# Writing out the slots of a windowed-attention and maxout kernel, each in its own order

## The chip, the cores and the metric

The kernel runs on one core of a Trainium2 chip. A core has five engines that run independently, each through its own instructions in a fixed order: TensorE (PE in the profile, with its weight loads as PEld), VectorE (DVE), ScalarE (ACT), GpSimd (POOL), and SyncE (SP), which here only issues DMAs. An instruction waits, if it must, on semaphores that other engines or DMAs raise, and everything behind it on its engine waits with it. The metric is the time of one execution in microseconds (us); the kernel before takes 179.16 us, the median of three runs (178.92 to 179.60).

## The reference

Two stages are computed one after the other.

```python
# q, k, v: (4 batches, 8 heads, 768 positions, 64); n_sink = 4, window = 128
scores = (q @ k^T) / sqrt(64)
keep = (key < n_sink) | (0 <= query - key < window)
a = softmax(where(keep, scores, -1e9))
x = (a @ v), heads side by side            # (3072 tokens, 512)
h = max(x @ w1, x @ w2, x @ w3)            # (3072, 768)
out = h @ w_out                            # (3072, 512)
```

## The kernel before

**Tiling.** The tokens are cut into twelve chunks of 256, three to a batch. A chunk's queries are two blocks of 128; a block sees the keys of its own block, of the block ahead of it, and the four sinks at the head of the batch. The work on chunk n is written as small helpers, each of which issues a few instructions:

- `load(n, 'k')`, `'q'`, `'v'` issue one DMA of 512 KB each on SP into raw float32 tiles, of which there are two for k, two for q and two for v. A `gate` puts a tiny GpSimd instruction ahead, so that the DMA waits for GpSimd's place in its own order.
- `cast_qk(n, w, g, engine)` casts half of k or q to bfloat16 on the engine named (4 per chunk); `cast_v(n, ...)` casts a quarter of v (4 per chunk).
- `turn(n, w, g)` and `turn2` transpose k or q with TensorE and a copy out of PSUM (chunks 0 to 3); `turn_dma(n, w)` does it with DMA transposes on SP (chunks 4 on; two DMAs for k into `kT`, one for q into `qT`).
- `score(n, pairs)` computes the scores of pairs of heads (four pairs, 0 to 3) into two PSUM banks per pair; `expo(n, p)` is ScalarE's two exponentials of a pair, which free the two banks; `mask(n, p)` multiplies by the 0/1 window mask on VectorE. In the first chunks `premask` lets TensorE write the mask into the bank ahead of the scores, in place of `mask`.
- `sink_k`, `sink_v` gather the sinks' keys (GpSimd) and values (a small TensorE product and a VectorE copy) once per batch; `sink_score(n)` scores them, `av_open(n)` opens the four output banks with the sinks' product. Chunks 0, 3, 6 and 9 need no sinks, since they lie at the head of a batch.
- `av(n, p)` multiplies by v, then VectorE divides by the sum (`rc` and `x_sb`, L359 and L362). `xpose` transposes x with TensorE, `xpose_dma(n)` with one DMA transpose on SP into `xT` (chunk 4 on).
- `ffn_h(n, fp, wi)`: eight matmuls for a third `fp` of h and one matrix `wi`; for `wi` = 0 ScalarE copies the bank into `h_sb` (L401), for 1 and 2 VectorE takes the maximum (L405). `ffn_y(n, t)`: six matmuls of half of the output and a copy, on ScalarE or on VectorE. `store(n)` writes it out.
- `warm(n)` is n matmuls on zeros, at the start.

**Order.** The order is written out by hand: each engine runs its instructions as the program text names them. From chunk 4 on the program runs in slots. I call slot n the stretch in which chunk n's scores are taken. In it TensorE also does the nine `ffn_h` of chunk n-1 and the two `ffn_y` of chunk n-2, while SP loads chunk n+2 and GpSimd casts it. Slots 4 and 11 and the stretch that follows 11 have their own branch in the loop; slots 5, 7, 8 and 10 share one, slots 6 and 9 share another.

**PSUM.** There are eight banks. `bank` takes the one that was freed longest ago in program order, and TensorE waits until whoever freed it is really done.

**The end of an execution** (the last slots) is the same text in both kernels.

Of the kernel before, what the change touches and what calls it, by code (L numbers as in the profile page):

```python
# [16 lines left out]
def kernel(  # L17
# [13 lines left out]
    nc = tc.nc  # L31
# [17 lines left out]
    with tc.manual_schedule():  # L49
# [445 lines left out]
        score(0, (1,))
        premask(1, (1,))
        turn2(1, 'k', 0, nc.vector)
        cast_qk(1, 'k', 1, nc.scalar)
        score(0, (3,))
        expo(0, 1)  # L500
        cast_qk(1, 'q', 1, nc.gpsimd)
        load(1, 'v')
        turn2(1, 'k', 1, nc.scalar)
        expo(0, 3)
        av_open(0)
        av(0, 0)
        av(0, 1)
        sink_v(0)
        turn2(1, 'q', 0, nc.vector)
        load_w(1, 0, 512)  # L510
        turn2(1, 'q', 1, nc.scalar)
        av(0, 2)
        av(0, 3)
        cast_v(1, 1, 1, nc.vector)
        score(1, (0,))
        expo(1, 0)
        sink_score(1)
        cast_v(1, 0, 1, nc.gpsimd)
# [7 lines left out]
        cast_v(1, 0, 0, nc.vector)  # L526
        premask(1, (3,))
        expo(1, 1)
        score(1, (3,))
        ffn_h(0, 2, 0)  # L530
        mask(1, 2)
        load(2, 'k', gate=after(0, 300))
        mask(1, 0)
        load_w(2, 512, 768)
        av_open(1)
        av(1, 2)
        av(1, 1)
        load_w(2, 0, 256)
        expo(1, 3)
        load(2, 'v', gate=after(1))  # L540
        av(1, 0)
        ffn_h(0, 1, 0)
        load(3, 'q', gate=after(0))
        av(1, 3)
        ffn_h(0, 0, 0)
        load_w(2, 256, 512)
        xpose(1, 1, nc.vector)
        xpose(1, 0, nc.scalar)
        ffn_h(0, 2, 1)
        cast_qk(2, 'q', 0, nc.gpsimd)  # L550
        load_wo(0, 3)
        ffn_h(1, 0, 0)
        ffn_h(1, 1, 0)
        load_wo(3, 6)
        ffn_h(1, 2, 0)
        load(3, 'k', gate=after(1))
        ffn_h(1, 0, 1)
        ffn_h(1, 1, 1)
        ffn_h(0, 0, 1)
        ffn_h(0, 1, 1)  # L560
        ffn_h(0, 2, 2)
        load(3, 'v', gate=after(2))
        cast_qk(2, 'k', 1, nc.scalar)
        cast_qk(2, 'k', 0, nc.gpsimd)
        cast_qk(2, 'q', 1, nc.vector)
        ffn_h(1, 2, 1)
        turn(2, 'q', 0, nc.scalar)
        ffn_h(1, 2, 2)
        turn(2, 'q', 1, nc.scalar)
        turn(2, 'k', 1, nc.vector)  # L570
        cast_v(2, 0, 1, nc.gpsimd)
        turn(2, 'k', 0, nc.vector)
        ffn_h(1, 0, 2)
        load(4, 'q')
        sink_score(2)
        score(2, (1,))
        load(4, 'k', gate=after(2))
        cast_v(2, 0, 0, nc.gpsimd)
        score(2, (2,))
        score(2, (3,))  # L580
        expo(2, 3)
        expo(2, 1)
        ffn_h(1, 1, 2)
        ffn_h(0, 0, 2)
        expo(2, 2)
        mask(2, 1)
        ffn_h(0, 1, 2)
        cast_v(2, 1, 1, nc.vector)
        cast_qk(3, 'q', 0, nc.gpsimd)
        cast_v(2, 1, 0, nc.vector)  # L590
        score(2, (0,))
        mask(2, 2)
        expo(2, 0)
        mask(2, 0)
        av_open(2)
        mask(2, 3)
        cast_qk(3, 'q', 1, nc.gpsimd)
        load(4, 'v', gate=pool_gate)
        ffn_y(1, 0)
        ffn_y(0, 0)  # L600
        cast_qk(3, 'k', 0, nc.scalar)
        av(2, 2)
        ffn_y(0, 1, nc.vector)
        av(2, 0)
        turn(3, 'q', 1, nc.scalar)
        turn(3, 'q', 0, nc.scalar)
        av(2, 3)
        av(2, 1)
        cast_qk(3, 'k', 1, nc.scalar)
        turn(3, 'k', 0, nc.scalar)  # L610
        cast_v(3, 1, 0, nc.vector)
        ffn_y(1, 1)
        cast_v(3, 1, 1, nc.gpsimd)
        turn(3, 'k', 1, nc.vector)
        xpose(2, 0, nc.scalar)
        xpose(2, 1, nc.vector)
        score(3, (0,))
        expo(3, 0)
        score(3, (3,))
        score(3, (1,))  # L620
        load(5, 'k')
        expo(3, 1)
        mask(3, 0)
        cast_v(3, 0, 0, nc.gpsimd)
        score(3, (2,))
        cast_v(3, 0, 1, nc.gpsimd)
        cast_qk(4, 'q', 1, nc.gpsimd)
        cast_qk(4, 'k', 1, nc.gpsimd)
        cast_qk(4, 'k', 0, nc.vector)
        ffn_h(2, 1, 0)  # L630
        expo(3, 2)
        expo(3, 3)
        ffn_h(2, 1, 1)
        cast_qk(4, 'q', 0, nc.gpsimd)
        mask(3, 1)
# [260 lines left out]
```

## Time and profile before

| | |
|---|---|
| median of three runs | 179.16 us (178.92 to 179.60) |
| the profiled execution | 179.04 us, its span 177.3 us |
| TensorE busy | 170.1 us, 96% of the span |
| VectorE / ScalarE / GpSimd busy | 126.5 / 85.8 / 67.1 us |
| mean granted TensorE clock | 0.996 |
| a slot (5, 7, 8, 10) | 13.1 to 13.2 us |
| a slot at the head of a batch (6, 9) | 12.5 us |

Busy time here is the time in which an engine has an instruction in hand. The span runs from the first to the last instruction; the time of an execution is some 1.7 us longer. A row of an order of time gives the start, the duration, the engine, the line of the kernel, the operation with output and input tiles and the number of instructions merged into the row; in brackets stand the idle time ahead of it and what ended that.

### The profile page before, as it was taken

What the parts mean: (1) busy time and instruction counts of PE and PEld (TensorE: products, weight loads), DVE (VectorE), ACT (ScalarE), POOL (GpSimd) and SP (SyncE); (2) the same over time, 40 slices, a digit from 0 to 9 for tenths busy, and PEclk for the clock granted to TensorE, in tenths of its full rate; (3) what the DMA queues carried; (4) which work ended last, traced back from release to release, by engine and by line L of the source; (5) the groups of instructions that cost most, each with busy time, mean ns of one, the idle gap of its engine ahead of it and who ended that gap; (6) DMA issues with size and microseconds to landing.
All of it is one profiled execution on the core that took longest, in us unless ns stands there. A gap on an engine that the chain in (4) does not pass through costs nothing.

```text
span 177.3 us, 4632 instructions
## 1 busy us (share of the span) xinstructions
PE 170.1 (96%) x1872; PEld 127.1 (72%) x1872; DVE 126.5 (71%) x267; ACT 85.8 (48%) x171; POOL 67.1 (38%) x123
## 2 busy tenths in 40 slices
PE   6899999999998999999999999999999999999991
PEld 2446889856895597697696696796795895796870
DVE  3389738699698578796884984975885875966451
ACT  3498732577924822913724814814616617320210
POOL 6884344146580274544724624417427000000000
PEclk9999999999999999999999999999999999999998
DMA  5999999995999969999999999999999519305203
GB/s 141 290 287 203 224 248 259 216 265 148 290 140 236 94 142 299 129 245 173 251 269 189 210 301 160 213 303 153 198 293 198 150 34 379 125 11 170 120 0 118
DMA packets 69573, 34.90 MB, mean 197 GB/s; under 512 B 26544, under 2 KB 68016, under 8 KB 69552
## 3 DMA queue, kind: packets, MB, share of 16 engines
q1 hardware_dynamic: 64912, 31.33, 81.3%
q0 software_dynamic: 4496, 3.15, 11.6%
q8 instruction: 14, 0.23, 0.5%
q10 hardware_dynamic: 144, 0.13, 0.2%
q14 instruction: 7, 0.06, 0.1%
HBM read 25.17 MB, written 6.29 MB: 177 GB/s over the span
## 4 chain that ended last, share of the span: by engine, by line
PE 87%; DMA 4%; DVE 3%; SPq 2%; POOL 1%; ACT 1%; issue 0%; POOLq 0%
PE h_ps L394 52%; PE y_ps L415 18%; PE o L354 6%; PE st L278 6%; DMA q_raw<-in_q_dram 4%; SPq L90 2%; DVE h_sb L405 1%; PE o L336 1%; PE sk L304 1%; PE pt L118 1%; PE y_ps L425 1%; DVE x_sb L362 1%; POOL q_bf L102 1%; PE xt L375 1%; DVE vb L108 0%
## 5 line engine op out<-in xcount | busy, mean ns | idle before, releaser
L394 PE MATMUL h_ps<-xT,w 128*128 128x256 bf16 x864 | 100.7, 273 | 0.1
L394 PEld LDWEIGHTS <-w 128*128 128x128 bf16 x864 | 82.2, 98 | 10.4 <-issue 0.5
L405 DVE TENSOR_TENSOR h_sb<-h_sb,h_ps 128x512 bf16<-128x512 bf16 (+1 forms) x74 | 49.2, 671 | 21.2 <-PE h_ps L394 19.4
L290 ACT ACTIVATE e_sb<-st 128x512 bf16<-128x512 f32 (+1 forms) x96 | 46.6, 579 | 5.9 <-PE st L278 5.8
L401 ACT CAST h_sb<-h_ps 128x512 bf16<-128x512 f32 x36 | 21.2, 588 | 43.1 <-PE h_ps L394 42.9
L108 POOL CAST vb<-v_raw 64x512 bf16<-64x512 f32 x38 | 28.0, 737 | 15.8 <-DMA v_raw<-in_v_dram 14.5
L296 DVE TENSOR_TENSOR e_sb<-e_sb,msk 128x1024 bf16<-128x1024 bf16 (+1 forms) x42 | 31.6, 786 | 2.5 <-ACT e_sb L290 2.3
L415 PE MATMUL y_ps<-wo,h_sb 128*128 128x512 bf16 x138 | 32.4, 379 | 0.2 <-DVE h_sb L405 0.2
L415 PEld LDWEIGHTS <-h_sb 128*128 128x128 bf16 x138 | 12.6, 98 | 14.8 <-issue 1.6
L362 DVE TENSOR_TENSOR x_sb<-o,rc 128x256 bf16<-128x256 f32 x48 | 20.4, 425 | 1.6
L102 POOL CAST k_bf<-k_raw 128x512 bf16<-128x512 f32 x17 | 10.3, 625 | 28.5 <-DMA k_raw<-in_k_dram 28.5
L102 POOL CAST q_bf<-q_raw 128x512 bf16<-128x512 f32 x21 | 13.3, 658 | 16.4 <-DMA q_raw<-in_q_dram 13.0
L417 DVE COPY y_sb<-y_ps 128x512 f32<-128x512 f32 x13 | 9.0, 691 | 13.7 <-PE y_ps L415 13.7
L354 PE MATMUL o<-vb,e_sb 128*128 128x65 bf16 x352 | 16.5, 193 | 0.0
L354 PEld LDWEIGHTS <-e_sb 128*128 128x128 bf16 x352 | 14.6, 97 | 2.0 <-DVE e_sb L296 0.2
L278 PE MATMUL st<-qT,kT 64*128 64x128 bf16 (+1 forms) x256 | 14.5, 238 | 0.5 <-ACT kT L125 0.5
L278 PEld LDWEIGHTS <-kT 64*128 64x128 bf16 x256 | 8.1, 94 | 7.1 <-issue 4.9
L310 ACT ACTIVATE e_sink<-sk 128x256 bf16<-128x256 f32 x8 | 3.1, 385 | 14.8 <-PE sk L304 14.8
L359 DVE RECIPROCAL rc<-o 128x4 f32<-128x4 f32 x48 | 8.4, 175 | 1.3 <-PE o L354 1.0
L417 ACT COPY y_sb<-y_ps 128x512 f32<-128x512 f32 x10 | 5.9, 586 | 3.3 <-PE y_ps L415 2.7
L102 ACT CAST k_bf<-k_raw 128x512 bf16<-128x512 f32 x5 | 3.1, 626 | 6.5 <-DMA k_raw<-in_k_dram 6.5
L180 PE MATMUL warm<-wz 128*128 128x512 bf16 x14 | 4.5, 462 | 1.2 <-DVE wz L169 1.2
(69 smaller groups left out, 72.7 us busy)
## 6 DMA issues: line engine op xcount, KB each, us to landing
k_raw<-in_k_dram SPq DMA_DIRECT2D x12, 512.0 KB, 5.5
q_raw<-in_q_dram SPq DMA_DIRECT2D x12, 512.0 KB, 7.0
v_raw<-in_v_dram SPq DMA_DIRECT2D x12, 512.0 KB, 8.2
out_dram<-y_sb SPq DMA_DIRECT2D x11, 512.0 KB, 4.0
w<-in_moe_w_dram POOLq DMA_DIRECT2D x5, 256.0 KB, 8.7
w<-in_moe_w_dram POOLq DMA_DIRECT2D x2, 512.0 KB, 9.8
wo<-in_moe_w_out_dram POOLq DMA_DIRECT2D x2, 384.0 KB, 9.8
kT<-k_bf SPq DMA_TRANSPOSE x16, 3.7
```

The costliest lines, as they stand in the source:

```text
L102: f(x[:, 2 * g:2 * g + 2].rearrange("q p i a d -> q p a i d"), y[:, 4 * g:4 * g + 4].rearrange("q (p a) i d -> q p a i d", a=2))
L108: eng.tensor_copy(vb[ci % RING][64 * i:64 * i + 64, n, :, 0:D], raws[ci, "v"][64 * n:64 * n + 64, :, i])
L278: nc.tensor.matmul(st[a][:, s:s + q1 - q0].rearrange("q n (i r) -> q n i r", i=2), lhsT=x[hp, n, p].rearrange("q i r -> q (i r)"), rhs=qc[ ...
L290: nc.scalar.activation(e[:, a, lo:], st[a][:, lo:], AF.Exp, scale=scale)
L296: (eng or nc.vector).tensor_mul(e[:, :, lo:], e[:, :, lo:], msk0 if lo else msk)
L354: nc.tensor.matmul(o[:, t, a], lhsT=e[:, a, s], rhs=vb[cv % RING][:, n, 2 * p + a], start=first, stop=True, skip_group_check=True)
L362: nc.vector.tensor_mul(xs[ci][:, :, p], o[:, :, :, 0:D], rc.unsqueeze(3).to_broadcast([128, 2, 2, D]))
L394: nc.tensor.matmul(hp[:, f].rearrange("q (i t r) -> q i t r", i=2, t=2), lhsT=w_sb[wi][:, ds, c0:c0 + 128], rhs=xTs[ci][:, :, ds].rearrang ...
L401: nc.scalar.copy(dst, hp)
L405: nc.vector.tensor_max(dst[:, x], dst[:, x], hp[:, x])
L415: nc.tensor.matmul(yp, lhsT=hs[ci][:, fb, t * 128:(t + 1) * 128], rhs=wo[:, fb], start=(fb == 0), stop=(fb == FB - 1))
L417: (nc.scalar.copy if eng is None else eng.tensor_copy)(ys[ci][:, t], yp)
```

## The change

Nothing that is computed changes, apart from four more `warm` matmuls (18 in place of 14). The order changes in four ways.

1. **Opening and chunks 0 to 3.** The helpers are called in another order. Twelve `warm` stand at the start and six after the last scores of chunk 0 (4, 9 and 1 before). `load(0, 'q')` has no gate now; `load(1, 'k')` is issued third, ahead of `load(0, 'v')`. Several casts of chunks 1 to 3 change their engine, and `load(4, 'k')` and `load(4, 'q')` change places.
2. **Slots 4 to 10 are written out.** The loop is gone. Before, all eight casts of the chunk ahead are on GpSimd. Now each has its place and engine: in slots 5, 7 and 8 three of the q and k casts are on ScalarE and one on VectorE, in slots 6 and 9 two on ScalarE, one on VectorE and one on GpSimd; the v casts stay on GpSimd there. Slot 4 casts both chunk 5 and chunk 6.
3. **Transfers.** The loads stay at the head of their slot, but what follows them is no longer `xpose_dma(n)`: in slots 5, 7, 8 and 10 it stands between the k and the q transposes of the chunk just loaded, in slots 6 and 9 behind both, and the store, which stood at the end of a slot, stands behind the loads.
4. **The sinks' v product**, `sink_v`, moves from slots 6 and 9 to slots 7 and 10, just ahead of their `sink_score`; `sink_k` moves to the end of slots 6 and 9.

SP's queue, slot 5 before. The numbers behind `kT` and `qT` are those of the ring of four tiles, so `kT_72` and `qT_76` belong to chunk 7 and `kT_69` and `qT_73` to chunk 8; `xT` is chunk 5's:

```order
L90 DMA k_raw<-in_k_dram 128x8x128
L90 DMA q_raw<-in_q_dram 128x8x128
L90 DMA v_raw<-in_v_dram 128x8x128
L381 DMA_TRANSPOSE xT<-x_sb 128x8x128
L162 DMA_TRANSPOSE kT_72<-k_bf 128x8x64 x2
L157 DMA_TRANSPOSE qT_76<-q_bf 128x8x128
L431 DMA out_dram<-y_sb 128x1024
```

SP's queue after, from the store of slot 5 to the end of slot 6:

```order
L431 DMA out_dram<-y_sb 128x1024
L162 DMA_TRANSPOSE kT_72<-k_bf 128x8x64 x2
L381 DMA_TRANSPOSE xT<-x_sb 128x8x128
L157 DMA_TRANSPOSE qT_76<-q_bf 128x8x128
L90 DMA k_raw<-in_k_dram 128x8x128
L90 DMA q_raw<-in_q_dram 128x8x128
L90 DMA v_raw<-in_v_dram 128x8x128
L431 DMA out_dram<-y_sb 128x1024
L162 DMA_TRANSPOSE kT_69<-k_bf 128x8x64 x2
L157 DMA_TRANSPOSE qT_73<-q_bf 128x8x128
L381 DMA_TRANSPOSE xT<-x_sb 128x8x128
```

In slot 5 the x transpose moved behind chunk 7's k, in slot 6 (the second `xT`) it moved behind both transposes of chunk 8.

VectorE, slot 5 before, from the copy of y to the first two maxima (`e_sb<-e_sb,msk` is `mask`, `rc` and `x_sb` are `av`, `h_sb<-h_sb,h_ps` is `ffn_h`):

```order
L417 COPY y_sb<-y_ps 128x512
L296 TENSOR_TENSOR e_sb<-e_sb,msk 128x1024 x3
L359 RECIPROCAL rc<-o 128x4
L362 TENSOR_TENSOR x_sb<-o,rc 128x2x128
L296 TENSOR_TENSOR e_sb<-e_sb,msk 128x1024
L359 RECIPROCAL rc<-o 128x4
L362 TENSOR_TENSOR x_sb<-o,rc 128x2x128
L405 TENSOR_TENSOR h_sb<-h_sb,h_ps 128x512 x2
```

The same stretch after:

```order
L296 TENSOR_TENSOR e_sb<-e_sb,msk 128x1024
L417 COPY y_sb<-y_ps 128x512 x2
L296 TENSOR_TENSOR e_sb<-e_sb,msk 128x1024
L359 RECIPROCAL rc<-o 128x4
L362 TENSOR_TENSOR x_sb<-o,rc 128x2x128
L102 CAST k_bf<-k_raw 128x2x2x2x64
L296 TENSOR_TENSOR e_sb<-e_sb,msk 128x1024
L405 TENSOR_TENSOR h_sb<-h_sb,h_ps 128x512
L296 TENSOR_TENSOR e_sb<-e_sb,msk 128x1024
```

A cast of k now stands ahead of the third mask, a maximum ahead of the fourth, and both halves of y are copied here.

ScalarE, slot 5 before (`e_sb<-st` is `expo`, `h_sb<-h_ps` is the copy of `ffn_h` with `wi` = 0):

```order
L310 ACTIVATE e_sink<-sk 128x256
L290 ACTIVATE e_sb<-st 128x512 x6
L417 COPY y_sb<-y_ps 128x512
L290 ACTIVATE e_sb<-st 128x512 x2
L401 CAST h_sb<-h_ps 128x512 x3
```

ScalarE, slot 5 after:

```order
L290 ACTIVATE e_sb<-st 128x512 x2
L310 ACTIVATE e_sink<-sk 128x256
L290 ACTIVATE e_sb<-st 128x512 x6
L102 CAST k_bf<-k_raw 128x2x2x2x64
L401 CAST h_sb<-h_ps 128x512 x2
L102 CAST q_bf<-q_raw 128x2x2x2x64
L401 CAST h_sb<-h_ps 128x512
L102 CAST q_bf<-q_raw 128x2x2x2x64
```

A copy of y left; a cast of k stands ahead of the first copies of h, a cast of q ahead of the last.

The diff, cut to the branch for slots 5, 7, 8 and 10 and to two of the slots that replace it:

```diff
-            elif n % CPB:
-                load(i + 3)
-                sink_score(n)
-                score(n, (0,))
-                expo(n, 0)
-                score(n, (3,))
-                score(n, (1,))
-                expo(n, 1)
-                expo(n, 3)
-                ffn_y(m, 0, nc.vector)
-                mask(n, 0)
-                ffn_y(m, 1)
-                score(n, (2,))
-                mask(n, 3)
-                av_open(n)
...
-                cast_qk(i + 3, 'k', 0, nc.gpsimd)
...
-                xpose_dma(n)
-                turn_dma(i + 3, 'k')
-                turn_dma(i + 3, 'q')
-                store(i - 4)
-                ffn_h(i, 2, 2, 1 if i + 2 < NCH else 2)
...
+        load(7, 'k')
+        load(7, 'q')
+        load(7, 'v')
+        score(5, (1,))
+        score(5, (0,))
+        expo(5, 0)
+        mask(5, 0)
+        score(5, (3,))
+        sink_score(5)
+        expo(5, 3)
+        ffn_y(3, 0, nc.vector)
+        expo(5, 1)
+        ffn_y(3, 1, nc.vector)
+        av_open(5)
+        score(5, (2,))
+        mask(5, 1)
+        expo(5, 2)
+        cast_qk(7, 'k', 0, nc.scalar)
+        store(0)
+        cast_v(7, 0, 0, nc.gpsimd)
+        av(5, 0)
+        ffn_h(4, 1, 0)
+        cast_qk(7, 'k', 1, nc.vector)
+        mask(5, 3)
+        ffn_h(4, 1, 2)
+        turn_dma(7, 'k')
+        ffn_h(4, 2, 0)
+        mask(5, 2)
+        cast_qk(7, 'q', 0, nc.scalar)
+        ffn_h(4, 0, 0)
+        av(5, 3)
+        av(5, 1)
+        ffn_h(4, 0, 2)
+        av(5, 2)
+        ffn_h(4, 0, 1)
+        xpose_dma(5)
...
+        turn_dma(7, 'q')
+
+        score(6, (1,))
+        load(8, 'k')
+        load(8, 'q')
+        load(8, 'v')
+        score(6, (0,))
+        expo(6, 0)
+        ffn_y(4, 0, nc.vector)
+        mask(6, 0)
+        expo(6, 1)
+        ffn_h(5, 1, 0)
+        score(6, (3,))
+        store(1)
+        cast_v(8, 1, 0, nc.gpsimd)
+        mask(6, 1)
+        cast_qk(8, 'q', 1, nc.gpsimd)
...
+        av(6, 0)
+        av(6, 1)
+        cast_qk(8, 'k', 1, nc.scalar)
+        turn_dma(8, 'k')
...
+        av(6, 2)
+        sink_k(2)
+        turn_dma(8, 'q')
+        xpose_dma(6)
+        ffn_y(4, 1)
```

More of the change, by code (lines that the diff above doesn't have):

```diff
@@ L522 @@
-        score(1, (2,))
         expo(1, 2)
@@ L574 @@
+        ffn_h(1, 2, 2)
+        ffn_h(0, 2, 2)
+        cast_v(2, 1, 0, nc.gpsimd)
         load(4, 'q')
-        sink_score(2)
+        mask(2, 2)
+        cast_qk(3, 'k', 1, nc.gpsimd)
         score(2, (1,))
[L577 to L593, printed above, removed]
         mask(2, 0)
         av_open(2)
+        expo(2, 1)
+        cast_qk(3, 'q', 1, nc.scalar)
+        ffn_y(0, 0)
+        mask(2, 1)
+        cast_v(3, 0, 1, nc.gpsimd)
         mask(2, 3)
[L597 to L600, printed above, removed]
+        load(4, 'v')
+        ffn_y(0, 1, nc.vector)
```

691 lines of the change are left out of this document (410 added, 281 removed).

## The prediction

> **What bounds the kernel now.** I read the page's first two parts, then the busy times by stage, then TensorE's order of time where a stage is not full, then the chain that ended last, for the pace of a slot, and SP's and GpSimd's order of time.
>
> ```profile
> PE 170.1 (96%) x1872; PEld 127.1 (72%) x1872; DVE 126.5 (71%) x267; ACT 85.8 (48%) x171; POOL 67.1 (38%) x123
> ```
>
> ```profile
> 0.00:14.00 14.00, 11.36 (x102) 5.74 (x103) 7.61 (x26) 8.00 (x17) 10.75 (x30) 1.00 1.00 237
> 44.00:58.00 14.00, 13.25 (x159) 10.49 (x156) 11.36 (x26) 8.30 (x18) 6.02 (x11) 1.00 1.15 226
> 95.20:108.40 13.20, 13.20 (x156) 10.01 (x156) 10.04 (x20) 6.68 (x13) 5.01 (x8) 1.00 1.11 222
> ```
>
> The columns are the stage, its length, then PE, PEld, DVE, ACT, POOL, the granted clock, the DMA share and GB/s. In slot 7 (95.2 to 108.4) TensorE is busy for all of its 13.20 us. Nothing can be won there except matmuls, and the change removes none. Only the opening and the stage from 44 to 58 are not full.
>
> ```profile
> 95.18 0.22 PE sk L304 x4
> 95.41 0.77 PE st L278 x18
> 96.17 2.69 PE y_ps L415 x12
> 103.50 0.48 PE o L354 x16
> 103.99 4.37 PE h_ps L394 x40
> 121.71 0.60 PE st L278 x12
> ```
>
> These pieces of the chain, which runs on TensorE alone there, give its prices: sink scores 0.22, a pair's scores 0.26 (0.77/3; 0.20 at the head of a batch), half of y 1.35, an `av` 0.24, an `ffn_h` 0.874 (4.37/5).
>
> ```profile
> 14.17 0.40 PE L278 MATMUL st<-qT,kT 64*128 64x128 bf16 x6
> 44.66 0.91 PE L278 MATMUL st<-qT,kT 64*128 64x256 bf16 x16
> 54.84 0.56 PE L375 MATMUL xt<-ident,x_sb 128*128 128x128 bf16 x7 [0.41 <-DVE x_sb L362]
> 56.62 0.59 PE L415 MATMUL y_ps<-wo,h_sb 128*128 128x512 bf16 x2 [0.22 <-DVE h_sb L405]
> 69.44 0.29 PE L304 MATMUL sk<-qT,ks 128*32 128x256 bf16 x4
> ```
>
> The first is where chunk 1's scores begin, 14.17; at that point both kernels have issued the same work. The third and fourth are TensorE's halts near the border of slots 3 and 4. From 44.66, where chunk 3's scores begin, to 69.44, the end of slot 4, the prices add up to 22.9 us (18 `ffn_h` 15.7, two halves of y 2.7, scores 1.8, `av` 1.7, the small ones 1.0), and it takes 24.8. So about 1.9 us are lost there, more than the idle entries say, since a busy matmul can be one that is held up.
>
> **The opening.** From the chain, and from the order of time of the warm matmuls' weight loads:
>
> ```profile
> 4.83 7.29 DMA q_raw<-in_q_dram
> 5.23 1.39 PEld L180 LDWEIGHTS <-wz 128*128 128x128 bf16 x7 [0.23 <-issue]
> ```
>
> Both kernels get chunk 1's q as the fifth load. It lands at 12.12 before, and nothing speeds it up now. I walked the new order by hand with before's durations. Twelve warm matmuls end near 5.7, before the first transposes can start; chunk 0's scores end near 10.1, six warm matmuls (0.20 each, 1.39/7) follow to 11.4, and TensorE then runs almost dense to chunk 1's scores at 14.1, against 14.17. I take -0.15 us for the stretch up to chunk 0's `ffn_h`, bounds -0.5 and +0.5, since filler of 1.2 us stands in front of real work.
>
> One wait is new. `ffn_h(0, 0, 2)` moves forward and needs w3's first 256 columns.
>
> ```profile
> 29.10 0.17 POOL L441 CAST v_raw<-w 1x1 f32<-1x1 bf16 x1 [1.27 <-DMA w<-in_moe_w_dram]
> ```
>
> GpSimd's gate is released by just this landing, near 29.05. In the new order TensorE would be there at 28.4; before, its first user of w3 needed the columns loaded ahead of these. That costs +0.4, bounds 0 and +0.7. Everything behind it on TensorE waits too.
>
> **Slots 3 and 4.** One thing that made VectorE late before the first halt leaves:
>
> ```profile
> 52.88 0.68 DVE L108 CAST vb<-v_raw 64x512 bf16<-64x512 f32 x1
> ```
>
> This v cast stands between the x of chunk 3 before and is GpSimd's now; the scores of chunk 3 also stand closer together. Walking VectorE's new order (mask 0.55, `rc` and x 0.60, maximum 0.69, all from rows below), the last x of chunk 3 is ready at 53.5 and TensorE arrives at 53.6; three of the four pairs of slot 4 are then held 0.1 to 0.3 us each by maxima that free their banks. I come to 23.6 us for the stretch in place of 24.8: -1.2, bounds -1.9 (all of the loss) and 0. The sum so far is -0.15 + 0.4 - 1.2 = -0.95.
>
> **Slots 5 to 10.** Work on TensorE is unchanged; `sink_v` moves its 0.18 us from slots 6 and 9 to 7 and 10. What is new is that q and k casts stand on ScalarE and VectorE among exponentials, masks and copies. On GpSimd they waited for a landing at nobody's cost.
>
> ```profile
> 97.32 1.25 SPq L157 DMA_TRANSPOSE qT<-q_bf  x1
> 99.02 0.35 SPq L431 DMA_DIRECT2D out_dram<-y_sb  x1
> 99.43 0.44 SPq L90 DMA_DIRECT2D k_raw<-in_k_dram  x1
> 101.01 1.70 SPq L90 DMA_DIRECT2D v_raw<-in_v_dram  x1
> 107.75 2.52 SPq L162 DMA_TRANSPOSE kT<-k_bf  x2
> 74.69 0.57 SPq L90 DMA_DIRECT2D k_raw<-in_k_dram  x1
> 79.86 1.24 SPq L381 DMA_TRANSPOSE xT<-x_sb  x1
> 79.40 1.17 POOL L102 CAST k_bf<-k_raw 128x512 bf16<-128x512 f32 x2 [2.51 <-DMA k_raw<-in_k_dram]
> 105.17 1.17 POOL L102 CAST k_bf<-k_raw 128x512 bf16<-128x512 f32 x2 [4.77 <-DMA k_raw<-in_k_dram]
> 109.73 2.98 POOL L108 CAST vb<-v_raw 64x512 bf16<-64x512 f32 x4 [0.75 <-DMA v_raw<-in_v_dram]
> ```
>
> ```profile
> L401 ACT CAST h_sb<-h_ps 128x512 bf16<-128x512 f32 x36 | 21.2, 588 | 43.1 <-PE h_ps L394 42.9
> L102 ACT CAST k_bf<-k_raw 128x512 bf16<-128x512 f32 x5 | 3.1, 626 | 6.5 <-DMA k_raw<-in_k_dram 6.5
> L102 DVE CAST k_bf<-k_raw 128x512 bf16<-128x512 f32 x2 | 0.9, 428 | 0.2 <-DMA k_raw<-in_k_dram 0.2
> L405 DVE TENSOR_TENSOR h_sb<-h_sb,h_ps 128x512 bf16<-128x512 bf16 x70 | 47.7, 686 | 20.9 <-PE h_ps L394 19.4
> L362 DVE TENSOR_TENSOR x_sb<-o,rc 128x256 bf16<-128x256 f32 x48 | 20.4, 425 | 1.6
> L359 DVE RECIPROCAL rc<-o 128x4 f32<-128x4 f32 x48 | 8.4, 175 | 1.3 <-PE o L354 1.0
> ```
>
> So k lands 4.7 us after its issue with no store ahead (74.69 to 79.40), 5.7 with one (99.43 to 105.17); v 8.7.
>
> *k in slots 5, 7 and 8.* Let k land L us after the slot's first score. Behind it stand VectorE's cast (0.43) and third mask (0.7), which `av(5, 3)` needs; TensorE is there after three pairs of scores, the sinks, y, one more pair, one `av` and four `ffn_h`, at 7.9. ScalarE's cast (0.63) and copy of h (0.59), then VectorE's maximum (0.69) and fourth mask (0.7), stand ahead of `av(5, 2)`, which TensorE reaches at 9.24. Both give about L = 6.65; each microsecond above stalls TensorE by one. SP reaches the load behind the transposes of the slot before: in slot 4 two pairs of k, two of q and x, which I count at 2.5, 1.25 and 1.24 each, and the k of chunk 6 waits for a GpSimd cast that stands behind v's landing. That puts the issue at 2.5 in slot 5, and by the same count at 2.8 in slot 7 and 1.2 in slot 8. I take 4.7 for the landing, as the nearer row, since the store now stands behind: L is 7.2, 7.5 and 5.9. Stalls: 0.55, 0.7 (`sink_v` gives 0.18 there) and 0. With 5.7 they would be 1.55, 1.65 and 0.25, together 3.45; with SP a microsecond earlier, 0. So +1.25, bounds 0 and +3.45.
>
> *x in slots 6 and 9.* `ffn_h(5, 1, 0)` moves up to behind two pairs of scores and one half of y, 1.74 us into slot 6. From the last `av` of slot 5 that is 5.23 us (four `ffn_h` and these); VectorE needs 2.2 of them for what stands ahead of the last x, SP 0.1, and the transpose has 2.9 left.
>
> ```profile
> DMA to landing us min/median/max: 3.0/4.9/5.8
> ```
>
> This is the row for `xT`; the shortest are those with no loads in flight, which is nearest to the new place, nine microseconds behind the loads. I take 3.1: +0.2 in each of slots 6 and 9, +0.4, bounds 0 and +4.0 (4.9 in both).
>
> *x behind the transposes, slots 7 and 10.* Slot 6 issues `xT` behind chunk 8's k and q transposes; half of its q is cast on GpSimd behind a v cast, so behind v's landing (8.7 after issue) and 1.4 us of casts (0.75, 2.98/4, and a q cast of much the same). That puts `xT` near 14 us and its landing near 17.1, when slot 7 needs it at 12.4 + 4.6 = 17.0. I take +0.3 for both slots, bounds 0 and +2.8.
>
> *Others.* ScalarE's casts of q wait for q, but the copies behind them have over 1 us to spare. The second copy of y (0.69) on VectorE in slots 5, 7, 8 and 10 lies beside TensorE's work: VectorE has 10.04 of 13.20 us in hand in slot 7, and would have 11.2. If that cover goes, the maxima behind run into the next slot and cost 0.69 at most. I take 0.
>
> Sum: 1.25 + 0.4 + 0.3 = +1.95 in the slots, -0.95 ahead of them, +1.0 in all. The profiled execution took 179.04; that gives 180.04, and 180.2 beside the median of 179.16, which lies 0.12 above it.
>
> **A rule against the row.** Masks with GpSimd's v casts beside them and without:
>
> ```profile
> 84.54 3.04 POOL L108 CAST vb<-v_raw 64x512 bf16<-64x512 f32 x4 [2.26 <-DMA v_raw<-in_v_dram]
> 85.56 2.43 DVE L296 TENSOR_TENSOR e_sb<-e_sb,msk 128x768 bf16<-128x768 bf16 x3
> 88.45 0.55 DVE L296 TENSOR_TENSOR e_sb<-e_sb,msk 128x768 bf16<-128x768 bf16 x1
> ```
>
> A mask takes 0.55 alone and 0.81 (2.43/3) beside the casts. The Trainium skill (SBUF — State Buffer, Who interferes with whom) says that a VectorE instruction with two inputs in SBUF and a GpSimd instruction that reads SBUF block each other, and that a VectorE cast can take the shared ports too. By that rule, which this row bears out for masks, taking casts off GpSimd would give up to 0.26 back per mask, and the two masks behind k's landing would bring the slots' sum from 1.95 to about 1.4. No row here shows a cast of VectorE holding GpSimd up. My sum stays with 0.7 per mask, between the two rows.
>
> **Rivals.** *Faster: every landing fits.* If SP is one microsecond earlier than I count, k lands at 6.2 and 6.5, all waits of the slots are 0 to 0.1, and the -0.95 stay: 178.2. For it speaks that each wait I found is under 0.8 us, so that a small error removes it; it decides at L = 6.65. Against it, that k's landing varied from 4.7 to 5.7 in the rows above.
>
> *Much slower: SP falls behind.* A late k delays the x transpose, which delays the loads of the next slot, on one queue. With 5.7 for k in all three slots, 4.9 for `xT` in one of 6 and 9, and 0.7 for the transposes in slots 7 and 10 together: 3.45 + 2.0 + 0.7 = 6.15; less the 0.95, +5.2, so 184.4 at the worst. The case begins at 181.5, and 183 is its middle. Against it speaks that v, the last of three loads, lands within 9 us of its issue, in a slot of 13.
>
> *The change does nothing by itself.* The halts at 54 to 57 stay (VectorE's chain there is only re-sorted) and the slots fit: 179.2 to 179.6.
>
> **How the numbers follow.** The forecast (179.5 to 181.5) has 0.42, the landings that fit 0.28, SP behind 0.15, no effect 0.15. Within 0.5% of before is about what a measurement of this kernel can tell from no change: 178.26 to 180.06. Faster: 0.22 of the second and 0.02 of luck in the others, 0.24. Same: 0.06 of the second, 0.12 of the fourth, 0.08 of the first, 0.26. Slower: the rest, 0.50. The range reaches from 178.0, where the second case gains a little more, to 183.0, which leaves the worst part of the third case out; the forecast's own range is 179.5 to 181.5.
>
> **What would show it.** In the profile after: ScalarE's and VectorE's casts of k waiting for the DMA of k in slots 5 and 7, and TensorE idle ahead of an `o` matmul (L354) by the same time; TensorE waiting for `xT` ahead of `h_ps` (L394) early in slots 6 and 9; slots 5 and 7 longer than 13.2 us; chunk 1's scores at 14.1; a wait for w near 28.4; slot 4 ending about 1 us earlier than 69.44. If slots 5 to 10 stay full, I am wrong on SP's place; if slot 4 ends no earlier, on VectorE's chain in slots 3 and 4.

## The result, and the profile after

The kernel after takes 182.12 us, the median of six executions (180.36 to 182.20); before takes 179.06 beside it (178.83 to 179.60). The ratio is 1.0145 with a 95% interval from 1.0104 to 1.0185: slower by 1.0 to 1.9%. Two further sets of the same kernel gave 181.25 (180.64 to 182.58) and 181.77 (180.98 to 182.08). Its executions differ by up to 2 us, those of before by 0.8 in the set beside it, so I read several of its profiles. The profiled execution that belongs to the result took 180.36 us, its span 178.6, 1.32 us more than the profiled execution of before.

The page's first part, and the windows that answer to those shown of before (44 to 58, then slots 5, 7 and 10 by their own bounds; columns as there):

```profile
PE 170.7 (96%) x1863; PEld 127.4 (71%) x1876; DVE 126.6 (71%) x278; ACT 93.6 (52%) x187; POOL 46.0 (26%) x95
```

```profile
44.00:58.00 14.00, 13.93 (x185) 11.88 (x184) 12.47 (x28) 9.60 (x22) 6.29 (x12) 1.00 0.91 208
68.69:82.93 14.24, 13.54 (x154) 9.90 (x154) 9.64 (x21) 8.16 (x16) 2.45 (x4) 1.00 1.04 213
95.25:109.14 13.89, 13.57 (x162) 10.04 (x162) 10.06 (x24) 8.16 (x16) 1.95 (x6) 1.00 1.11 218
134.58:148.45 13.87, 13.59 (x161) 10.26 (x160) 10.13 (x23) 6.71 (x13) 0.81 (x3) 1.00 0.66 88
```

The stage from 44 to 58 has filled up (13.93 us busy where it was 13.25). Three of the slots that were full, at 13.1 to 13.2 us, have become 13.9 to 14.2 long, and TensorE is not busy for all of them. GpSimd has 21 us less of work, ScalarE 8 more, VectorE as much as before.

TensorE's order of time shows where. The rows are the wait for w3, chunk 3's scores, the starts of slots 5, 7, 8, 10 and 11, and the two waits for x:

```profile
29.10 1.92 PE L394 MATMUL h_ps<-xT,w 128*128 128x256 bf16 x16 [0.48 <-DMA w<-in_moe_w_dram]
45.24 0.90 PE L278 MATMUL st<-qT,kT 64*128 64x256 bf16 x16
68.69 0.84 PE L278 MATMUL st<-qT,kT 64*128 64x128 bf16 x18
73.97 3.67 PE L394 MATMUL h_ps<-xT,w 128*128 128x256 bf16 x32 [0.62 <-DMA xT<-x_sb]
95.25 0.84 PE L278 MATMUL st<-qT,kT 64*128 64x128 bf16 x18
109.14 0.84 PE L278 MATMUL st<-qT,kT 64*128 64x128 bf16 x18
134.58 0.84 PE L278 MATMUL st<-qT,kT 64*128 64x128 bf16 x18
139.76 3.67 PE L394 MATMUL h_ps<-xT,w 128*128 128x256 bf16 x32 [0.23 <-DMA xT<-x_sb]
148.45 0.29 PE L304 MATMUL sk<-qT,ks 128*32 128x256 bf16 x4
```

The chain of work that ended last now leaves TensorE twice for a load of k, which it never did in these slots before:

```profile
71.98 4.52 DMA k_raw<-in_k_dram
...
76.63 0.10 DVE k_bf L102
...
76.97 0.70 DVE e_sb L296
...
77.71 0.66 PE o L354 x16
...
98.19 4.53 DMA k_raw<-in_k_dram
...
102.84 0.10 DVE k_bf L102
...
103.18 0.69 DVE e_sb L296
...
103.92 0.66 PE o L354 x16
```

It is the path of the prediction, in slots 5 and 7: the load, VectorE's cast of k, the mask behind it, and the `av` that needs the mask. In slot 10 the chain leaves TensorE for the transpose of x instead (issued at 135.21, landed 4.51 later).

I take a slot from its first score, sink score or sinks' v product on TensorE to that of the next (before, slots 6 and 9 begin with the `sink_v` that the change moves). The lengths, in us, in the profiled executions that the rest speaks of (each of these has its granted clock at 1.00 in all six slots; "all mended" and "new front, x ahead" are two of the experiments, the latter the last one below):

| kernel | slot 5 begins | 5 | 6 | 7 | 8 | 9 | 10 |
|---|---|---|---|---|---|---|---|
| before | 69.44 | 13.17 | 12.50 | 13.18 | 13.17 | 12.50 | 13.17 |
| after | 68.69 | 14.24 | 12.32 | 13.89 | 13.17 | 12.27 | 13.87 |
| after, repeated | 68.57 | 14.45 | 12.33 | 15.09 | 13.18 | 12.26 | 14.78 |
| after, third set | 68.54 | 14.77 | 12.33 | 13.94 | 13.18 | 12.26 | 14.62 |
| all mended | 68.66 | 13.18 | 12.27 | 13.47 | 13.17 | 12.27 | 13.79 |
| new front, x ahead | 68.55 | 13.17 | 12.50 | 13.18 | 13.17 | 12.50 | 13.18 |

So the whole loss is in slots 5, 7 and 10. Slots 6 and 9 are shorter by the `sink_v` that left, and slot 8 is as it was.

### The profile page after: what moved, and what is told of

It is laid out like the page before. It is cut to its first block, busy times and chain, and to the rows that moved or that the text cites. A ratio compares the mean times of both kernels' runs of the same rounds, so it can differ in the third digit from the quotient of the medians.

```text
span 178.6 us, 4646 instructions
## 1 busy us (share of the span) xinstructions
PE 170.7 (96%) x1863; PEld 127.4 (71%) x1876; DVE 126.6 (71%) x278; ACT 93.6 (52%) x187; POOL 46.0 (26%) x95
## 4 chain that ended last, share of the span: by engine, by line
PE 64%; DMA 19%; DVE 6%; ACT 5%; issue 2%; POOL 1%; SPq 0%; DVEq 0%; POOLq 0%
PE h_ps L394 40%; PE y_ps L415 12%; DMA w<-in_moe_w_dram 8%; DMA k_raw<-in_k_dram 5%; PE o L354 4%; PE st L278 4%; ACT e_sb L290 4%; DMA q_raw<-in_q_dram 3%; DMA xT<-x_sb 3%; DVE h_sb L405 2%; DVE x_sb L362 1%; PE pt L118 1%; DVE e_sb L296 1%; PE y_ps L425 1%; ACT h_sb L401 1%
## 5 line engine op out<-in xcount | busy, mean ns | idle before, releaser
L290 ACT ACTIVATE e_sb<-st 128x512 bf16<-128x512 f32 (+1 forms) x96 | 46.5, 581 | 14.1 <-PE st L278 12.2
L108 POOL CAST vb<-v_raw 64x512 bf16<-64x512 f32 x37 | 23.7, 643 | 65.2 <-DMA v_raw<-in_v_dram 52.3
L296 DVE TENSOR_TENSOR e_sb<-e_sb,msk 128x1024 bf16<-128x1024 bf16 (+1 forms) x42 | 27.0, 661 | 6.9 <-ACT e_sb L290 6.8
L415 PEld LDWEIGHTS <-h_sb 128*128 128x128 bf16 x138 | 12.6, 98 | 13.9 <-issue 0.8
L417 DVE COPY y_sb<-y_ps 128x512 f32<-128x512 f32 x16 | 11.1, 691 | 8.3 <-PE y_ps L415 7.9
L354 PEld LDWEIGHTS <-e_sb 128*128 128x128 bf16 x352 | 13.9, 98 | 2.6 <-DVE e_sb L296 0.8
L278 PE MATMUL st<-qT,kT 64*128 64x128 bf16 (+1 forms) x256 | 14.1, 238 | 0.1
L102 ACT CAST q_bf<-q_raw 128x512 bf16<-128x512 f32 x17 | 10.6, 630 | 5.2 <-DMA q_raw<-in_q_dram 5.0
L417 ACT COPY y_sb<-y_ps 128x512 f32<-128x512 f32 x7 | 4.1, 585 | 13.9 <-PE y_ps L415 13.9
L102 ACT CAST k_bf<-k_raw 128x512 bf16<-128x512 f32 x8 | 4.9, 617 | 10.1 <-DMA k_raw<-in_k_dram 10.0
L102 DVE CAST k_bf<-k_raw 128x512 bf16<-128x512 f32 x10 | 4.8, 484 | 4.6 <-DMA k_raw<-in_k_dram 4.6
L180 PE MATMUL warm<-wz 128*128 128x512 bf16 x17 | 6.6, 552 | 1.2 <-DVE wz L169 1.2
L102 POOL CAST k_bf<-k_raw 128x512 bf16<-128x512 f32 x6 | 3.9, 652 | 11.0 <-PE h_ps L394 5.6
```

The costliest lines, as they stand in the source:

```text
L102: f(x[:, 2 * g:2 * g + 2].rearrange("q p i a d -> q p a i d"), y[:, 4 * g:4 * g + 4].rearrange("q (p a) i d -> q p a i d", a=2))
L108: eng.tensor_copy(vb[ci % RING][64 * i:64 * i + 64, n, :, 0:D], raws[ci, "v"][64 * n:64 * n + 64, :, i])
L278: nc.tensor.matmul(st[a][:, s:s + q1 - q0].rearrange("q n (i r) -> q n i r", i=2), lhsT=x[hp, n, p].rearrange("q i r -> q (i r)"), rhs=qc[ ...
L290: nc.scalar.activation(e[:, a, lo:], st[a][:, lo:], AF.Exp, scale=scale)
L296: (eng or nc.vector).tensor_mul(e[:, :, lo:], e[:, :, lo:], msk0 if lo else msk)
L354: nc.tensor.matmul(o[:, t, a], lhsT=e[:, a, s], rhs=vb[cv % RING][:, n, 2 * p + a], start=first, stop=True, skip_group_check=True)
```

## The experiments

**The change again.** The kernel as it is, for a second profile of it.

> The changed kernel once more, unchanged. Its profiled execution was the fastest of six (180.36 us; the median is 182.12), so 1.8 us of the usual loss stand in no profile yet. Theory 1 (k's landing in front of masks and copies): in a usual execution k lands about 1 us later in slots 5 and 7, both are near 15 us, and ScalarE and VectorE wait for k there; times 181 to 182.2. Theory 2 (the x transposes come late on SP's queue): the two extra microseconds are TensorE waiting for xT early in slots 7 and 10. If it is neither, the opening or slots 3 and 4 vary.

It took 181.25 us (180.64 to 182.58), ratio 1.0124 (1.0088 to 1.0161). The profile is of the longest of these executions, 182.58 us, and both kinds of wait of the expectation stand in it. Slot 5 takes 14.45 us, slot 7 takes 15.09, and in slot 7 TensorE waits first for x and then for the mask behind k:

```profile
100.82 3.67 PE L394 MATMUL h_ps<-xT,w 128*128 128x256 bf16 x32 [0.53 <-DMA xT<-x_sb]
105.22 0.66 PE L354 MATMUL o<-vb,e_sb 128*128 128x65 bf16 x16 [0.73 <-DVE e_sb L296]
```

GpSimd's and TensorE's order of time also shows a wait that I had not foreseen:

```profile
134.00 0.61 POOL L108 CAST vb<-v_raw 64x512 bf16<-64x512 f32 x1 [10.30 <-DMA v_raw<-in_v_dram]
134.68 0.61 POOL L102 CAST q_bf<-q_raw 128x512 bf16<-128x512 f32 x1
135.24 1.93 POOL L108 CAST vb<-v_raw 64x512 bf16<-64x512 f32 x3
137.21 0.43 POOL L233 COPY ks<-kT 64x16 bf16<-64x16 bf16 x2
137.70 0.29 PE L304 MATMUL sk<-qT,ks 128*32 128x256 bf16 x4 [0.80 <-POOL ks L233]
```

`sink_k(3)` now stands at the end of slot 9, behind GpSimd's casts of v(11), and these wait for v's landing. The copy needs nothing of v; it is only queued behind it, and slot 10's sink scores wait for it.

**One half at a time.** First the new front (opening to the end of slot 4) with slots 5 to 11 of the kernel before:

```diff
         <opening to slot 4 of the kernel after>
-        load(7, 'k')
-        load(7, 'q')
...
+        for i in range(4, NCH):
+            <the loop of the kernel before>
```

> The new opening and slots up to the end of slot 4, then before's slots 5 to 11. Both theories place the loss in slots 5 to 10 and a gain of 0.75 us ahead of them (slot 4 ends at 68.69 in place of 69.44), so 178.3 us. If it is 179 or more, the gain ahead is given back behind; if it is above 180, the usual 1.8 us come from the opening.

178.90 us (178.48 to 179.55), ratio 0.9983 (0.9972 to 0.9993). TensorE began slot 5 at 68.36, 1.08 earlier than before, and gave 0.78 of it back in that slot, which took 13.95 us:

```profile
73.64 1.91 PE L394 MATMUL h_ps<-xT,w 128*128 128x256 bf16 x16 [0.62 <-DMA xT<-x_sb]
```

This x is chunk 4's. Its transpose stands at the end of slot 4 behind chunk 6's k and q transposes, which I had counted for the loads behind them, but not for x itself.

Then the front of the kernel before with the new slots:

> Before's opening and slots up to slot 4, then the new slots 5 to 11. Theory 1: the loads of chunk 7 are issued at 74.7, 5.2 us into slot 5, so k lands at 9.9 and stalls TensorE for 9.9 - 6.65 = 3.3 us there; with 0.5 each in slots 7 and 10 and no gain ahead that is 183.4 us (182.5 to 184.5). Theory 2: k's landing costs little, slots 7 and 10 lose 0.5 to 1 each, 180.5 us.

183.42 us (182.22 to 184.07), ratio 1.0218 (1.0181 to 1.0254). TensorE, VectorE and ScalarE in slot 5, and the same stretch by windows:

```profile
78.67 0.62 ACT L102 CAST k_bf<-k_raw 128x512 bf16<-128x512 f32 x1 [3.61 <-DMA k_raw<-in_k_dram]
78.69 0.43 DVE L102 CAST k_bf<-k_raw 128x512 bf16<-128x512 f32 x1 [3.40 <-DMA k_raw<-in_k_dram]
79.77 0.89 PE L354 MATMUL o<-vb,e_sb 128*128 128x65 bf16 x16 [1.99 <-DVE e_sb L296]
```

```profile
77.78:79.77 1.99, 0.00 (x1) 0.00 (x1) 1.03 (x2) 1.10 (x3) 0.00 (x0) 1.00 1.21 293
79.77:83.25 3.48, 3.48 (x36) 2.81 (x37) 3.09 (x8) 2.11 (x4) 0.98 (x2) 0.54 1.21 315
```

The slots carry the loss and k's landing is its place, as theory 1 has it, and the number is met; but part of it comes by a path that the expectation doesn't have, so the number is met partly by luck. Slot 5 took 16.97 us, 3.80 more than before. The wait for k accounts for 2.2 (worked out in the next section). The rest, 1.6, is the clock: behind a pause of 1.99 us TensorE was granted 0.54 for 3.48 us, and 3.48 times 0.46 is 1.6. Of its four executions the two with a mean clock of 0.991 took 183.8 and 184.1, the two at 1.0 took 182.2 and 183.0. So the slow clock did not come in every execution.

**The casts back on GpSimd.** The changed kernel with all q and k casts of slots 5 to 9 on GpSimd, together at the place of the first:

```diff
-        cast_qk(7, 'k', 0, nc.scalar)
+        cast_qk(7, 'k', 0, nc.gpsimd)
+        cast_qk(7, 'k', 1, nc.gpsimd)
+        cast_qk(7, 'q', 0, nc.gpsimd)
+        cast_qk(7, 'q', 1, nc.gpsimd)
...
-        cast_qk(7, 'k', 1, nc.vector)
```

> The changed kernel with all four casts of q and k of slots 5 to 9 on GpSimd, together, where the first cast of the slot stood; all else as it is. Theory 1: no cast waits for a landing on ScalarE or VectorE any more; the waits ahead of av in slots 5 and 7 go, 0.6 to 0.7 left for xT in slot 5, 179.0 to 179.6 us. Theory 2: the waits for xT stay, 181 to 182.

179.95 us (179.73 to 180.26), ratio 1.0040 (1.0025 to 1.0056). So 1.3 of the 2.0 us by which the repeated set (181.25) lies above before (179.25) hang on the casts. Their engine and their place changed together here; the next run keeps both. The executions agree again within 0.6 us; I take it, without a run that shows it, that this is because no landing stands ahead of masks. The median is 0.35 above the expectation, for x: slot 5 took 14.35 us, slot 6 12.82.

```profile
74.22 3.67 PE L394 MATMUL h_ps<-xT,w 128*128 128x256 bf16 x32 [0.98 <-DMA xT<-x_sb]
85.20 1.05 PE L394 MATMUL h_ps<-xT,w 128*128 128x256 bf16 x8 [0.38 <-DMA xT<-x_sb]
```

**k loaded earlier, casts where the change has them.**

```diff
+        load(7, 'k')
         turn_dma(6, 'k')
...
-        load(7, 'k')
         load(7, 'q')
```

and the same for `load(9, 'k')` ahead of `turn_dma(8, 'k')`.

> The changed kernel with two loads of k issued earlier: chunk 7's stands ahead of chunk 6's k and q transposes at the end of slot 4, chunk 9's ahead of chunk 8's at the end of slot 6. Slot 8 keeps its order. Theory 1 (the time goes to k landing in front of masks and copies): the casts of k in slots 5 and 7 no longer wait for the DMA, slot 7 takes 13.2 to 13.3 us, slot 5 at most 13.9 (the wait for x of chunk 4, 0.6, is left), and the median falls by 0.9 to 1.3 us, to 180.0 to 180.4. Theory 2 (the casts cost time by where they stand, whatever the landing: copies and maxima behind them free their banks later): slots 5 and 7 stay at 14.2 and 13.8 or more, and the median stays at 181.2 to 182.1.

180.56 us (179.57 to 182.94), ratio 1.0071 (1.0043 to 1.0099). In slot 5 of its profiled execution (179.57) the casts wait for nothing, and x is what is late:

```profile
73.63 3.67 PE L394 MATMUL h_ps<-xT,w 128*128 128x256 bf16 x32 [0.39 <-DMA xT<-x_sb]
73.89 0.62 ACT L102 CAST k_bf<-k_raw 128x512 bf16<-128x512 f32 x1
74.13 0.42 DVE L102 CAST k_bf<-k_raw 128x512 bf16<-128x512 f32 x1
```

Slot 5 took 13.74 us, slot 7 13.47. That is theory 1 in its mechanism: the same casts at the same places cost little once k is there. The median is 0.2 above theory 1's range, since slot 10 (14.17) and three executions that took over 181 are left. The longest of these, 182.94, had a mean granted clock of 0.991, as the two long ones of the run with the old front and the new slots had; 0.009 of 182.94 is 1.6 us, by my estimate its loss to a slow stretch like the one there. It has no profile, nor have the other two, at 0.998.

**The sinks' keys earlier, and x ahead of q.** Two edits, first each alone:

```diff
+        sink_k(3)
         cast_v(11, 1, 0, nc.gpsimd)
...
-        sink_k(3)
```

> The changed kernel with the gathering of the sinks' keys (GpSimd) moved from the end of slots 6 and 9 to the place ahead of those slots' v casts. If the wait of the sink scores of slot 10 for that copy, 0.80 us in the repeated execution, is a cost by itself: no wait for ks ahead of them, slot 10 shorter by that much, and the median lower by 0.4 to 0.8 us, 180.4 to 181.0 where the changed kernel has 181.25 to 182.1. If it only shows a lateness that TensorE would meet at another wait a little later (the x transpose behind the same transposes), the median falls by less than 0.2 us and the wait for xT in slot 10 grows.

```diff
+        xpose_dma(9)
         turn_dma(11, 'q')
-        xpose_dma(9)
```

> The changed kernel with the x transpose of slots 6 and 9 moved ahead of the q transpose of the chunk just loaded. If x waits there for its place in SP's queue: the waits for xT in slots 7 and 10 (0.53 and 0.38 us in the repeated execution) are gone and the median falls by 0.5 to 0.9 us, since the transpose leaves at least 1.3 us earlier; the q transpose and the next loads come no later. If x waits for the transposes and loads in flight beside it, which share the DMA engines, it lands no earlier and the median stays within 0.2 us.

The first gave 181.21 us (180.25 to 182.04), ratio 1.0117 (1.0085 to 1.0150), the second 181.57 (180.92 to 183.58), ratio 1.0147 (1.0110 to 1.0183). Neither can be told from the unchanged kernel. With the keys early, slot 10 waits for x:

```profile
140.27 3.67 PE L394 MATMUL h_ps<-xT,w 128*128 128x256 bf16 x32 [0.68 <-DMA xT<-x_sb]
```

With x ahead of q, the wait for x is gone in slots 7 and 10, and others have its place, k's mask in slot 7 and the sinks' keys in slot 10:

```profile
104.93 0.66 PE L354 MATMUL o<-vb,e_sb 128*128 128x65 bf16 x16 [1.20 <-DVE e_sb L296]
137.56 0.29 PE L304 MATMUL sk<-qT,ks 128*32 128x256 bf16 x4 [0.95 <-POOL ks L233]
```

For the keys the second outcome of the expectation is met. For x the expected gain didn't come, although x was earlier: a wait on TensorE is worth only what it sticks out beyond the next one.

Both edits together:

> The changed kernel with both of the edits that gained nothing alone: the sinks' keys are gathered ahead of the v casts of slots 6 and 9, and the x transpose of these slots stands ahead of the q transpose. Theory 1 (the two waits in slot 10 lie one behind the other on TensorE, and k's late landing in slot 7 lies behind the wait for x; each hides the next): slot 10 takes 13.35 to 13.4 us, where it took 13.87 to 14.78, and slot 7, whose k is not mended, stays at 13.8 to 15.0; the median falls by 0.7 to 1.1 us against the unchanged kernel beside it. Theory 2 (slot 10 is late for something further, such as the k transposes of chunk 11): slot 10 stays above 13.8 with a third wait, and the median falls by less than 0.4.

181.42 us (180.75 to 182.05) beside 181.77 for the unchanged kernel on the same chip; the intervals of the two ratios (1.0086 to 1.0139, and 1.0097 to 1.0156) overlap. Slot 10 took 14.02 us, so theory 2 is nearer: something further is late. ScalarE's and SP's order of time in slot 9, and TensorE in slot 10:

```profile
131.94 0.62 ACT L102 CAST q_bf<-q_raw 128x512 bf16<-128x512 f32 x1 [2.20 <-DMA q_raw<-in_q_dram]
132.47 0.61 ACT L102 CAST k_bf<-k_raw 128x512 bf16<-128x512 f32 x1
133.11 2.52 SPq L162 DMA_TRANSPOSE kT<-k_bf  x2
136.07 1.23 SPq L381 DMA_TRANSPOSE xT<-x_sb  x1
140.77 1.31 PEld L394 LDWEIGHTS <-w 128*128 128x128 bf16 x13 [0.49 <-DMA xT<-x_sb]
```

ScalarE's second half of k stands behind its half of q, which waits for q; the k transposes wait for that cast, and x's transpose for them on SP. It was issued 0.63 us into slot 10 (136.07, the slot begins at 135.44) and landed some 4.7 later.

**Everything mended at once.** The three edits above, and slot 4's x transpose ahead of chunk 6's q transpose. The casts stay on ScalarE and VectorE.

```diff
+        xpose_dma(4)
         turn_dma(6, 'q')
-        xpose_dma(4)
```

> The changed kernel with everything that the theory blames mended and nothing else: the loads of k for chunks 7 and 9 earlier, the sinks' keys gathered earlier, the x transposes of slots 6 and 9 ahead of q's, and the x transpose of slot 4 ahead of chunk 6's q transpose. The casts of q and k stay on ScalarE and VectorE. If the list of causes is complete, slots 5, 7, 8 and 10 take 13.2 to 13.4 us, slot 5 begins at 68.4 to 68.7, and the time is that of the new front alone without its wait for x: 178.0 to 178.8. If a cause is missing, some slot stays above 13.6 us and the median above 179.2.

178.71 us (178.04 to 179.83), ratio 0.9970 (0.9951 to 0.9990); the unchanged kernel beside it took 181.77. Slot 5 is at 13.18, slot 7 at 13.47, slot 8 at 13.17. Slot 10, at 13.79, is outside the expectation, with x issued 0.62 us into it:

```profile
133.64 1.23 SPq L381 DMA_TRANSPOSE xT<-x_sb  x1
138.12 3.67 PE L394 MATMUL h_ps<-xT,w 128*128 128x256 bf16 x32 [0.15 <-DMA xT<-x_sb]
```

Slots 5 to 10 together take 78.15 us, where they took 77.69 before, 79.76 in the result's profile and 81.10 in the third set's. So the list of causes holds all but 0.46 us, and 3 us are given back without moving a single cast to another engine.

> The changed kernel as it is, beside the three above on the same chip: 180.4 to 182.6, the median near 181.5 to 182.1. It is there as the mark for the differences, since its executions differ by up to 2 us.

181.77 us (180.98 to 182.08), ratio 1.0127 (1.0097 to 1.0156).

**The new front, mended.** With the slots of the kernel before, chunk 6's q transpose behind slot 4's x transpose; first together with w3's first 256 columns ahead of its last:

```diff
-        turn_dma(6, 'q')
...
         xpose_dma(4)
+        turn_dma(6, 'q')
```

```diff
+        load_w(2, 0, 256)
         load_w(2, 512, 768)
...
-        load_w(2, 0, 256)
```

> The new opening and slots up to the end of slot 4 in front of slots 5 to 11 of the kernel before (178.9 us), with two further edits: chunk 6's q transpose stands behind the x transpose of slot 4, and w3's first 256 columns are loaded ahead of its last 256. If the 0.6 us that slot 5 waited for x of chunk 4 came from the q transpose ahead of it on SP, that wait goes; if the wait for w3 near 29 us is one for the order of the two weight loads, it goes too (about 0.4), unless the columns loaded second are then late. Both gone: 177.9 to 178.2 us. Only x: 178.3. If x lands late for another reason (its transpose shares the DMA engines with the loads): 178.8 to 179.0.

178.37 us (177.93 to 178.58), ratio 0.9948 (0.9932 to 0.9964). The waits for x and for w3 were both gone, but one for the output weights, which are issued behind those columns, had come:

```profile
38.41 0.81 PE L415 MATMUL y_ps<-wo,h_sb 128*128 128x512 bf16 x3 [0.45 <-DMA wo<-in_moe_w_out_dram]
```

Then without the exchange of the loads:

> The new front with slots 5 to 11 of the kernel before, and chunk 6's q transpose behind the x transpose of slot 4; the two loads of weights are left in the new front's order. In the run with both edits the wait for w3 went, but one of 0.45 us for the output weights came at 38.41 and chunk 3's scores began 0.43 us later (45.34 for 44.91). If the exchange of the loads only moved the wait: 177.9 to 178.1. If it was harmless and slot 5 began later for another reason: 178.3 to 178.4, as with both edits.

178.15 us (178.06 to 178.26), ratio 0.9932 (0.9911 to 0.9954): the lowest median here. It is 0.05 above the range for "the exchange only moved the wait". From the run with the exchange (0.9932 to 0.9964) it can't be told by the ratios; in the profiles slot 5 begins at 68.55 without it and at 68.79 with it. Slot 5 takes 13.17. Against the new front alone the move of one transpose gave back 0.75 of the 178.90, and these two intervals lie apart.

## Why the prediction was right, and where it was not

The forecast was 180.2 us, slower through waits for landings in slots 5 to 10. The direction and the cause hold, and the median, 182.12, is inside the whole range of 178.0 to 183.0. But it is outside the forecast's own range, 179.5 to 181.5: the change costs 3.06 us where 1.0 was forecast. The profiled execution took 180.36, and the working gave 180.04 for one. That closeness is partly luck. It was the fastest of six, and its slots 5 to 10 cost 2.07 us more than before (79.76 - 77.69), for a forecast 1.95, because slot 5 cost more than forecast and slots 6 and 9 nothing. In the repeated profile they cost 4.40, in the third set's 3.41. So the sum of the slots was too small, in two terms: when k lands in slots 5 and 7, and how long the transposed x of slot 10 takes to land. In the order of the prediction:

- **Opening, -0.15:** right. Chunk 1's scores came at 14.12 (14.1 forecast).
- **The wait for w3, +0.4:** right in the result's profile, 0.48; it was 0.30 in the repeated one, and the third set's order of time shows none. The mended front shows that its removal only lets the output weights be late.
- **Slots 3 and 4, -1.2:** right in size; no run takes the v cast away alone, so its share is not shown. From chunk 3's scores to slot 5, 45.24 to 68.69, it took 23.45 us (23.6 forecast, 24.8 before). The whole front gave -0.75 in that profile and -1.08 with the old slots, for -0.95.
- **k in slots 5, 7 and 8, +1.25:** the mechanism was right, the size too small in slot 5. The rule "every microsecond of L above 6.65 stalls TensorE by one" holds with the threshold at 6.87, read off these profiles: with VectorE's cast starting at L, the slot is longer than 13.17 by L - 6.87 in each of them.

| slot 5 of | L | L - 6.87 | longer by |
|---|---|---|---|
| after | 76.63 - 68.69 = 7.94 | 1.07 | 1.07 |
| after, repeated | 76.72 - 68.57 = 8.15 | 1.28 | 1.28 |
| after, third set | 77.01 - 68.54 = 8.47 | 1.60 | 1.60 |
| new slots, old front | 78.69 - 69.63 = 9.06 | 2.19 | 3.80, of it 1.6 by the clock |

  L was 7.2 in the forecast. What failed is the time of issue: 2.5 us into the slot by my count of SP's queue, 3.3 by the trace (71.98 - 68.69), since the last transposes of chunk 6's k start only when GpSimd has cast its second half (in the third set from 65.62 to 66.42; SP issues the transposes at 66.44), and q's and x's transposes stand in between. The landing then took 4.5 to 5.1, where I took 4.7. In slot 7 a half of y waits 0.17 for a bank that ScalarE's exponentials free, and the slot takes 13.47 without any wait for k (with `sink_v`'s 0.18); its stall was 0.42 in the result's profile and 1.62 in the repeated one (from the cast, at 102.84 and 104.14, to the slot's end it is 6.30 in both, as in slot 5), where k was issued 3.6 us into the slot (98.94) and landed in 5.1; 0.7 forecast. Slot 8 was right, 0 with the load at 1.1.
- **x in slots 6 and 9, +0.4:** wrong, 0. Both slots are shorter by the `sink_v` that left and no more. It was close in slot 6 of the result's profile: the transpose issued at 81.30 landed 3.4 later, and TensorE's first `ffn_h` of it starts at 84.71.
- **x behind the transposes, +0.3 for slots 7 and 10:** in slot 7 the k behind it hides it. In slot 10 it sets the time, and it was mis-sized: 0.40 in the result's profile, 1.31 in the repeated one, the wait of 0.80 for the sinks' keys included (above the 13.47 that slot 10 takes with `sink_v` and y's wait, taken from slot 7). I took 3.1 us from issue to landing. These are the rows for x of the transfers' view of after (median us from issue to landing at the end), first in slot 7, then in slot 10:

```profile
xT<-x_sb SPq DMA_TRANSPOSE x1, 3.2
```

```profile
xT<-x_sb SPq DMA_TRANSPOSE x1, 4.5
```

  In slot 10 it took 4.5 in each profile of the unchanged kernel. Why there and not in slot 7 stays open. In slot 10 a store stands behind it, where slot 7 has loads, and the next transpose of x in the result's profile, at 146.20 and also with a store behind it, took 4.6. But the store is not the whole cause: the transpose at 144.31 in the profile of before has a store right behind it too and took 3.0, and in the three runs that put q's transpose between x and the store, x of slot 10 still took 4.4 to 5.0.
- **Not in the list at all:** the wait for x of chunk 4 in slot 5 (0.62, hidden by k's in the changed kernel, a cost of its own in the new front) and the sinks' keys behind v (up to 0.95; with the keys early, slot 10 waited for x).
- **y's second copy, 0:** right; no profile puts a wait of TensorE down to it.

Of the rivals, "every landing fits" (178.2) describes the changed kernel once the loads and transposes are in time: 178.71. "SP falls behind" began at 181.5, and 10 of the 16 executions of the changed kernel are above that, as are two of its three medians. The repeated profile shows its way: the load of k is issued 3.59 us into slot 7 there, 2.94 in the result's profile, and k lands 1.2 later in the slot. It had 0.15 and should have had more, though it stayed below its middle of 183.

The rule of the Trainium skill (SBUF — State Buffer, Who interferes with whom) agrees with the groups of the masks, before and after, as fewer of GpSimd's casts lie beside them:

```profile
L296 DVE TENSOR_TENSOR e_sb<-e_sb,msk 128x1024 bf16<-128x1024 bf16 x30 | 23.3, 812 | 1.6 <-ACT e_sb L290 1.5
L296 DVE TENSOR_TENSOR e_sb<-e_sb,msk 128x768 bf16<-128x768 bf16 x12 | 8.3, 722 | 0.9 <-ACT e_sb L290 0.9
```

```profile
L296 DVE TENSOR_TENSOR e_sb<-e_sb,msk 128x1024 bf16<-128x1024 bf16 x30 | 20.3, 694 | 5.4 <-ACT e_sb L290 5.3
L296 DVE TENSOR_TENSOR e_sb<-e_sb,msk 128x768 bf16<-128x768 bf16 x12 | 6.7, 576 | 1.6 <-ACT e_sb L290 1.5
```

The mean mask fell from 812 to 694 ns at this width. It gave nothing to the two masks behind k's landing, though: they took 0.68 to 0.70, which is what a mask of this width takes alone (0.68 at 101.41 in the profile of before, with no cast of GpSimd beside it), and my 0.7 was already that. The 1.4 that I worked out by the rule rested on rows of the smaller width.

## What to carry to other kernels

A cast of freshly loaded data may wait for a DMA at nobody's cost on an engine that has little else to do; on an engine whose next instructions feed TensorE, every microsecond past a fixed point of the slot is paid, so work out that point and the load's time of issue from the queue ahead of it before moving the cast. Waits of an engine that follow one another hide each other: mending one shows nothing until the others are mended too, so try them together before calling one harmless. On one DMA queue, put the transfer that is needed first ahead, even if another is ready earlier: here the order of two transposes was worth 0.75 us.

## What the runs showed of the hardware

A pause of TensorE can cost more than itself. In the run with the old front and the new slots, a pause of 1.99 us was followed by 3.48 us at a granted clock of 0.54, which made the loss 3.8 us in place of 2.2. A pause of 1.20 us, in slot 7 with x ahead of q, was followed by the full clock. Two windows of that kernel, the pause and what follows it:

```profile
103.00:105.00 2.00, 0.80 (x9) 0.48 (x8) 1.07 (x3) 1.18 (x3) 0.00 (x0) 1.00 1.23 300
105.00:107.00 2.00, 2.00 (x37) 1.77 (x38) 1.93 (x6) 1.83 (x4) 0.00 (x0) 1.00 1.10 345
```

The length of the slow stretch agrees with the window of about 3.4 us of busy work after which, by the Trainium skill (TensorE: Matmul & The Clock Gate, What's actually happening), the full clock is granted; the pause that brought it, 1.99 us, was shorter than the idle window of about 3.4 us named there. The other half of that run's executions has a mean clock of 1.0, and no profile, so no run tells whether such a pause always brings the slow clock, from what length on, and whether the moment matters.
